# Attention and two expert layers on one core: a scheduler is told that three weight loads land later

## The chip, the core and the metric

The kernel runs on one core of a Trainium2 chip. The metric is the time of one execution on the device in microseconds, as the median of several runs. Engines are named as the profile names them: PE is TensorE (matmuls), PEld its weight loads, DVE VectorE, ACT ScalarE, POOL GpSimd and SP SyncE, whose queue issues the transfers (DMA). Each engine takes its instructions in the order in which the program emits them.

## What is computed

Three layers, one behind the other, in float32:

```python
for t in range(S):                       # attention: B=2, H=8, S=768, D=40
    C = f_stab * C + i_stab * outer(v[t], k[t]);  n = f_stab * n + i_stab * k[t]
    y[t] = sigmoid(o_gate[t]) * (C @ q[t]) / max(|n . q[t]|, 1)
x = y as 1536 tokens x 320
x = sum over 4 experts of p[:, e] * (relu(x @ w1[e]) @ w2[e])      # w1 320x1024, w2 1024x320
e = argmax(x @ w_gate), gate = softmax there                       # 8 experts, at most 384 tokens each
out[i] = gate[i] * (relu(x[i] @ w1[e]) @ w2[e])  for tokens that found a place, else 0
```

The first expert layer is called moe (experts k = 0 to 3), the second moe2 (k = 4 to 11, so k = 8 is moe2's expert 4).

## The kernel before

**Staging.** The attention is done in 12 units of 128 tokens, on PE up to about 200 us. Each unit leaves a token tile in xT. moe begins while the attention runs, an expert's tile at a time: layer 1 (L1, 128 matmuls of 128 columns in four quads at L652, or groups of four tiles in matmuls of 512 columns, also L652, with a closing half at L661), then layer 2 (L2, L674). Between them a bank is emptied twice: ACT takes the relu (L681), DVE the part that 16 bits have cut off (L683). DVE adds an expert's result to the accumulator (L715).

**Weights.** An expert's weights come from DRAM as float32 by `w_load`, w1 in three parts of 512 KB and w2 in two halves of 640 KB, into one buffer for each (`raw`). ACT passes over each piece for its largest value (L529), POOL reduces over the partitions, DVE spreads the result (L563) and makes a scale from it (L444 to L456). Then ACT (L597) and DVE (L602) split the weights into two 16-bit halves. Experts k = 8 to 11 come first in the order, and their halves are stored in DRAM and fetched again later (L506).

**Routing.** When a tile has its last moe expert, it is scaled and split (L633), transposed (by a transfer on SP, L640, or for the last three tiles by PE, L1432), and multiplied with the gate (L1441). PE counts how many tokens precede each one in its expert (L1467, L1468), and POOL scatters the rows into `disp` in DRAM. From there SP reads them back transposed (L1561 for three early expert tiles, L1768 for the window, which is the bulk of moe2). The results go out by indirect stores from POOL.

**What sets the order.** The kernel doesn't emit as it goes. Every operation is recorded by `Sched.add` with an engine, a cost in us and its dependencies. `Sched.starts` plays the program through with these costs and gives each operation a planned start; `run` emits the operations in order of planned start. A planned time isn't a measured one. It decides only what stands ahead of what in an engine's queue. Planned transfers of 1.44 to 1.9 us (the weight loads, 1.46 and 1.82) that end behind 165 us are taken to land `LOADS[0]` = 1.0 us later than the plain sum. Semaphores are derived from the dependencies, so that any order is right.

Of the kernel before, what the change touches and what calls it, by code (L numbers as in the profile page):

```python
# [67 lines left out]
LOADS = (1.0, 165.0)  # L68


class Sched:
# [86 lines left out]
    def starts(self, lst):  # L158
# [13 lines left out]
        while count < n:  # L172
            t, e = min((max(free[e], min(est[i] for i in c)), e) for e, c in ready.items() if c)
            i = min((i for i in ready[e] if est[i] <= t + self.HOLD[e]), key=lambda i: (i not in self.now, lst[i], i))
            ready[e].remove(i)
            if e == "DMA" and len(lanes) >= 8 and t < lanes[-8]:
                free[e] = lanes[-8]
                ready[e].append(i)
                continue
            start[i] = max(t, est[i])  # L180
            us = ops[i][1]
            count += 1
            free[e] = end = start[i] + us
            if e == "DMA":
                if ops[i][0] == "DMA":
                    free[e] = start[i] + 0.43
                    end = pipe = max(pipe, free[e]) + (us if us >= 0.8 else 0.15)
                else:
                    end = pipe = max(pipe, end)
                lanes.append(end + 1.7)  # L190
            if e == "DMA" and 1.44 < ops[i][1] < 1.9 and end > LOADS[1]:
                end += LOADS[0]
            for q in users[i]:
                est[q] = max(est[q], end + self.lag(ops[i][0], ops[q][0]) + self.care(ops[i][0], ops[q][0], end) + (SLACK if q in self.late else 0.0))
                left[q] -= 1
                if not left[q]:
                    ready.setdefault(unit[q], []).append(q)
# [1865 lines left out]
```

## Time and profile before

| | |
|---|---|
| median of 3 runs | 491.23 us (490.77 to 492.03) |
| profiled execution | 491.25 us, of which span 489.5 us |
| granted TensorE clock | 1.0 of full speed |
| PE busy | 473.4 us (97% of the span) |
| DVE, ACT, POOL busy | 342.4, 311.8, 144.5 us |
| moved by DMA | 89.10 MB |

The span is the time from the first to the last instruction of the profiled execution; the 1.75 us beside it are start and end. Busy is the time in which an engine had an instruction at work. Matmuls are pipelined and their ends are modelled. In timelines and waits, "a <-ACT b" is idle time that the named instruction ended.

### The profile page before, as it was taken

How to read it: one execution, taken by the hardware profiler on the slowest of the kernel's cores; microseconds unless marked ns; L12 is line 12 of the kernel's file. 1: busy time of each engine (PE TensorE's matmuls, PEld its weight loads, DVE VectorE, ACT ScalarE, POOL GpSimd, SP SyncE). 2: the span in 40 equal slices, each digit the busy share in tenths (PEclk: the TensorE clock that was granted, in tenths of full speed). 3: DMA queues.
4: the chain of work that ended last, by engine and by line, in shares of the span. 5: the costliest groups of instructions: out<-in, count | busy, mean ns of one | idle time of the engine just before them, and what ended most of it. 6: DMA issues, size and time to landing. Idle time of an engine off the chain costs nothing.

```text
span 489.5 us, 13777 instructions
## 1 busy us (share of the span) xinstructions
PE 473.4 (97%) x5469; PEld 363.0 (74%) x5469; DVE 342.4 (70%) x1008; ACT 311.8 (64%) x666; POOL 144.5 (30%) x297
## 2 busy tenths in 40 slices
PE   8999999999989899999999999999999999999995
PEld 6998978868878798887464646565564798978884
DVE  5898998799999934764978795679989882222110
ACT  1997979577687854866665678788978451312221
POOL 4742152664875420301102101010514121311111
PEclk9999999999999999999999999999999999999999
DMA  7996783354543796928887776627393464989301
GB/s 225 318 240 200 161 288 77 72 131 103 105 61 67 213 338 210 191 78 298 300 265 274 268 253 264 192 73 207 112 221 56 91 260 76 301 194 311 137 16 35
DMA packets 71588, 89.10 MB, mean 182 GB/s; under 512 B 49457, under 2 KB 57123, under 8 KB 71518
## 3 DMA queue, kind: packets, MB, share of 16 engines
q1 hardware_dynamic: 70318, 84.43, 60.6%
q0 software_dynamic: 1200, 3.73, 2.3%
q8 instruction: 45, 0.74, 0.6%
q14 instruction: 25, 0.20, 0.1%
HBM read 55.89 MB, written 21.70 MB: 159 GB/s over the span
## 4 chain that ended last, share of the span: by engine, by line
PE 51%; DVE 23%; DMA 17%; issue 6%; ACT 3%; POOL 0%; POOLq 0%; ACTq 0%; DVEq 0%; SPq 0%
PE po L674 20%; PE ph L652 14%; DMA out_dram<-acc,usm 9%; PE x L652 9%; DMA arena<-arena 3%; DVE arena L683 3%; DVE w L602 3%; DMA raw<-in_moe_w_dram 3%; DVE arena L1196 2%; DMA arena<-in_att_dram 2%; DVE arena L1066 2%; PE x L674 1%; PE ph L420 1%; ACT junk L529 1%; DVE usm L1005 1%
## 5 line engine op out<-in xcount | busy, mean ns | idle before, releaser
L674 PEld LDWEIGHTS <-arena 128*128 128x128 f16 (+1 forms) x1416 | 136.8, 98 | 53.9 <-issue 2.0
L652 PEld LDWEIGHTS <-w 128*128 128x128 f16 x1792 | 97.1, 98 | 5.0 <-issue 3.9
L652 PE MATMUL ph<-xT,w 128*128 128x128 f16 (+3 forms) x1664 | 96.2, 217 | 2.1 <-DVE arena L683 1.1
L652 PEld LDWEIGHTS <-arena 128*128 128x128 f16 x936 | 62.1, 98 | 39.6 <-issue 1.5
L674 PE MATMUL po<-arena 128*128 128x320 f16 x648 | 90.3, 299 | 0.0
L674 PE MATMUL po<-w,arena 128*128 128x320 f16 (+1 forms) x600 | 86.3, 299 | 1.4 <-DVE acc L715 1.3
L529 ACT ACTIVATE junk<-raw 128x512 bf16<-128x512 f32 (+1 forms) x105 | 69.7, 664 | 8.3 <-DMA raw<-in_moe_w_dram 6.6
L683 DVE SCALAR_TENSOR_TENSOR arena<-ph,arena 128x512 f16<-128x512 f32 x76 | 51.5, 682 | 15.0 <-ACT arena L681 14.9
L597 ACT ACTIVATE w<-raw,wsm 128x640 f16<-128x640 f32 (+1 forms) x56 | 50.4, 960 | 15.5 <-DVE wsm L451 15.5
L602 DVE SCALAR_TENSOR_TENSOR w<-raw,wsm,w 128x640 f16<-128x640 f32 (+1 forms) x56 | 57.1, 1049 | 4.3 <-ACT w L597 4.2
L681 ACT ACTIVATE arena<-ph 128x512 f16<-128x512 f32 x76 | 44.5, 588 | 20.4 <-PE ph L652 12.8
L652 PE MATMUL ph<-xT,arena 128*128 128x128 f16 (+4 forms) x472 | 57.5, 275 | 0.0
L652 PE MATMUL x<-xT,arena 128*128 128x128 f16 (+4 forms) x464 | 56.0, 274 | 0.0
L548 POOL CROSS_LANE_REDUCE wsm<-wsm 128x1 f32<-128x6 f32 (+1 forms) x24 | 9.7, 402 | 101.2 <-ACT junk L529 82.5
L602 DVE SCALAR_TENSOR_TENSOR arena<-raw,wsm,arena 128x640 f16<-128x640 f32 (+1 forms) x28 | 30.5, 1101 | 1.9 <-ACT arena L597 1.8
L715 DVE SCALAR_TENSOR_TENSOR acc<-po,cfs,acc 128x320 f32<-128x320 f32 x36 | 19.6, 545 | 14.8 <-PE po L674 13.5
L703 POOL TENSOR_TENSOR cfs<-pw,invx 128x1 f32<-128x1 f32 x48 | 17.8, 402 | 35.5 <-DVE invx L456 30.9
L597 ACT ACTIVATE arena<-raw,wsm 128x640 f16<-128x640 f32 (+1 forms) x28 | 25.7, 955 | 2.9 <-DVE wsm L451 2.9
L1806 POOL DMA_INDIRECT out_dram<-acc,usm x13 | 12.7, 974 | 48.4 <-ACT acc L1803 46.5
L681 ACT ACTIVATE arena<-x 128x512 f16<-128x512 f32 x26 | 14.5, 593 | 15.5 <-PE x L652 8.5
L1213 POOL TENSOR_TENSOR arena<-arena 128x512 f16<-128x512 f32 x16 | 20.6, 1304 | 12.1 <-ACT arena L1209 12.1
L1800 DVE SCALAR_TENSOR_TENSOR arena<-x,arena 128x512 f16<-128x512 f32 (+1 forms) x10 | 6.5, 652 | 25.2 <-ACT arena L1795 25.2
(245 smaller groups left out, 676.7 us busy)
## 6 DMA issues: line engine op xcount, KB each, us to landing
raw<-in_moe_w_dram SPq DMA_DIRECT2D x36, 512.0 KB
raw<-in_moe_w_dram SPq DMA_DIRECT2D x24, 640.0 KB
ws<-w SPq DMA_DIRECT2D x8, 768.0 KB
ws<-w SPq DMA_DIRECT2D x8, 640.0 KB
arena<-in_att_dram SPq DMA_DIRECT2D x8, 492.0 KB
disp<-zero SPq DMA_DIRECT2D x1, 3936.0 KB
arena<-ws SPq DMA_DIRECT2D x4, 768.0 KB
arena<-ws SPq DMA_DIRECT2D x4, 640.0 KB
```

The source lines that it names most:

```text
L529: nc.scalar.activation(out=junk[:, 0:w], in_=raw[:, i * w:(i + 1) * w], func=AF.Abs, accum_out=am[:, i:i + 1])
L597: lambda sl=sl: nc.scalar.activation(out=wh[:, sl], in_=raw[:, sl], func=AF.Copy, scale=sc),
L602: lambda sl=sl: nc.vector.scalar_tensor_tensor(wl[:, sl], raw[:, sl], sc, wh[:, sl], ALU.mult, ALU.subtract),
L652: nc.tensor.matmul(out=out, lhsT=wb[wi][:, c, f * 128:(f + 1) * 128], rhs=rhs(xc), start=(i == 0), stop=(i == LAST))
L674: nc.tensor.matmul(out=po[0:n, 0:DM], lhsT=hs[:, f, sl], rhs=ws[:, f, :], start=(f == 0 and i == 0), stop=(f == NF - 1 and i == 2),)
L681: act(0.52, lambda: nc.scalar.activation(out=hh, in_=ph, func=AF.Relu), [kp] + ex, [kh])
L683: 0.6, lambda: nc.vector.scalar_tensor_tensor(hl, ph, 0.0, hh, ALU.max, ALU.subtract),
L703: 0.26, lambda: nc.gpsimd.tensor_tensor(cf, pw[:, t, k:k + 1], invx[:, t:t + 1], ALU.mult),
L715: lambda: nc.vector.scalar_tensor_tensor(acc[:, t], po[:, 0:DM], cf, acc[:, t], ALU.mult, ALU.add),
L1066: lambda x=x, hi=hi, lo=lo, src=src: nc.vector.scalar_tensor_tensor(lo, src, sc[:, x:x + 1], hi, ALU.mult, ALU.subtract), [kr2, ks, key("h ...
L1213: 1.3, lambda j=j: nc.gpsimd.tensor_tensor(Wl[:, j::2], pb[:, j::2], Wh[:, j::2], ALU.subtract),
L1806: nc.gpsimd.indirect_dma_start(out=view_of(), out_offset=bass.IndirectOffsetOnAxis(ap=ix[0:n], axis=0), in_=acc[0:n, y], in_offset=None, b ...
```

## The change

One number in the scheduler's model: weight loads whose planned end lies between 191 and 205 us are taken to land 3.0 instead of 1.0 us behind the plain sum.

```diff
             if e == "DMA" and 1.44 < ops[i][1] < 1.9 and end > LOADS[1]:
-                end += LOADS[0]
+                end += LOADS[0] + (2.0 if 191.0 < end < 205.0 else 0.0)
             for q in users[i]:
```

Three loads fall in these bounds: the third part of w1 and both halves of w2 of expert k = 8. No instruction is added and none is left out, and no queue gets another kind of work. What moves is the order, from 205 to about 405 us behind the start.

On ACT, where expert k = 8's weights arrive (raw_87 is the buffer of w2, raw_86 that of w1, ph_97 and ph_98 are banks of layer 1); - is before, + is the change:

```order
 L681 ACTIVATE arena<-ph_97 128x512
 L529 ACTIVATE junk,wsm<-raw_86 128x512 x5
+L529 ACTIVATE junk,wsm<-raw_87 128x640
+L681 ACTIVATE arena<-ph_98 128x512
+L529 ACTIVATE junk,wsm<-raw_87 128x640
+L681 ACTIVATE arena<-ph_97 128x512
 L529 ACTIVATE junk,wsm<-raw_87 128x640 x2
-L681 ACTIVATE arena<-ph_98 128x512
-L529 ACTIVATE junk,wsm<-raw_87 128x640
-L681 ACTIVATE arena<-ph_97 128x512
-L529 ACTIVATE junk,wsm<-raw_87 128x640
 L681 ACTIVATE arena<-ph_98 128x512
```

The relu of bank ph_98 stood behind two passes over w2 and stands behind one; that of ph_97 stood behind three and stands behind two.

On PE, at the same place (x_102 is a bank that a group of four tiles of expert k = 2 uses, w_89 holds 16-bit weights of w1, po_100 a bank of layer 2):

```order
 L674 LDWEIGHTS arena
 L674 MATMUL po_100<-w_91,arena 128x320
+L652 LDWEIGHTS arena
+L652 MATMUL x_102<-xT,arena 128x512
...
 L652 LDWEIGHTS w_89
 L652 MATMUL ph_98<-xT,w_89 128x128
```

Seven such pairs, one block of layer 1, stand now ahead of the run of 128 matmuls on ph_98 and ph_97. Before, they stood behind that run and the 96 matmuls of layer 2 that follow it.

On DVE, behind the loads' arrival, the order of a bank's second emptying and of the scale of w2:

```order
 L715 SCALAR_TENSOR_TENSOR acc<-po_100,cfs,acc 128x320
 L683 SCALAR_TENSOR_TENSOR arena<-ph_97,arena 128x512
-L683 SCALAR_TENSOR_TENSOR arena<-ph_98,arena 128x512
-L563 STREAM_SHUFFLE wsm<-wsm 128x1
-L444 TENSOR_SCALAR wsm<-wsm 128x1
+L563 STREAM_SHUFFLE wsm<-wsm 128x1
+L444 TENSOR_SCALAR wsm<-wsm 128x1
+L683 SCALAR_TENSOR_TENSOR arena<-ph_98,arena 128x512
 L446 TENSOR_SCALAR wsm<-wsm 128x1
```

The emptying of ph_98 stands now behind two instructions of the scale.

Behind that the orders agree again up to the routing, from about 325 us on. There most engines' queues differ: sums and emptyings come ahead of weight splits of k = 5 to 7. On SP, the end of that stage (raw_87 and raw_86 loads of k = 6 and 7, L640 the transposes of token tiles):

```order
+L426 DMA raw_86<-in_moe_w_dram 128x1024 x3
+L640 DMA_TRANSPOSE arena<-arena 128x5x128
+L426 DMA raw_87<-in_moe_w_dram 128x1280
+L640 DMA_TRANSPOSE arena<-arena 128x5x128
 L426 DMA raw_87<-in_moe_w_dram 128x1280
 L640 DMA_TRANSPOSE arena<-arena 128x5x128 x2
-L426 DMA raw_87<-in_moe_w_dram 128x1280
-L640 DMA_TRANSPOSE arena<-arena 128x5x128 x2
-L426 DMA raw_86<-in_moe_w_dram 128x1024 x3
-L426 DMA raw_87<-in_moe_w_dram 128x1280 x2
-L640 DMA_TRANSPOSE arena<-arena 128x5x128 x4
```

Before, all five loads of k = 7 stood ahead of the last four transposes. In the change the first of these transposes stands behind the three loads of w1 and ahead of both of w2.

On PE, near the end of the routing (L1520 and L1467 count tokens, po_100 is a half of layer 2 of the first early tile, which runs under a branch, L1591):

```order
 L1520 LDWEIGHTS call
 L1520 MATMUL x_102<-run,call 128x8
-L1591 COMPARE_AND_BRANCH
-L674 LDWEIGHTS arena
-L674 MATMUL po_100<-arena 128x320
...
-L1591 UNCONDITIONAL_BRANCH x2
-L1467 LDWEIGHTS call
```

In the change these 12 matmuls stand one quad of layer 1 earlier, ahead of the count of token tile 9. The counts of tiles 10 and 11 have also one more block ahead of them, a quad of layer 1 or a half of layer 2 of the next early tiles.

## Rows read from the trace of the kernel before

**Rows 1.** The page: busy us (share of the span) and instructions of an engine.

```profile
PE 473.4 (97%) x5469; PEld 363.0 (74%) x5469; DVE 342.4 (70%) x1008; ACT 311.8 (64%) x666; POOL 144.5 (30%) x297
```

**Rows 2.** Waits of PE, 200 to 480 us: us in total, times, longest.

```profile
PE po L1840 <- issue: 1.2, 1, 1.2
PE ph L652 <- DVE arena L683: 0.9, 1, 0.9
PE x L652 <- issue: 0.5, 1, 0.5
PE x L1441 <- DMA arena<-arena: 0.4, 1, 0.4
```

**Rows 3.** The chain of waits, 198 to 236 us: start, us, what.

```profile
201.15 7.28 DMA raw<-in_moe_w_dram
...
208.52 0.84 ACT junk L529 x2
...
209.38 0.83 ACT junk L529 x2
210.21 0.49 ACT arena L681
...
210.72 0.70 DVE arena L683
...
231.81 1.51 PE ph L652 x7
```

**Rows 4.** Timeline of PE, 203 to 240 us: start, us, instruction.

```profile
207.19 3.42 PE L674 MATMUL po<-w,arena 128*128 128x320 f16 x24
211.47 7.31 PE L652 MATMUL ph<-xT,w 128*128 128x128 f16 x128 [0.86 <-DVE arena L683]
...
236.28 0.39 PE L661 MATMUL ph<-xT,arena 64*128 64x512 f16 x1
```

**Rows 5.** Timeline of DVE, 186 to 220 us.

```profile
202.25 0.88 DVE L602 SCALAR_TENSOR_TENSOR arena<-raw,wsm,arena 128x640 f16<-128x640 f32 x1
...
214.70 0.15 DVE L563 STREAM_SHUFFLE wsm<-wsm 128x1 f32<-128x1 f32 x1
214.89 0.15 DVE L444 TENSOR_SCALAR wsm<-wsm 128x1 f32<-128x1 f32 x1
```

**Rows 6.** Timeline of PE, 360 to 416 us.

```profile
366.23 0.28 PE L1441 MATMUL x<-wg,arena 128*128 128x16 f16 x5 [0.41 <-DMA arena<-arena]
...
392.38 0.27 PE L1441 MATMUL x<-wg,arena 128*128 128x16 f16 x5
...
398.81 1.79 PE L674 MATMUL po<-arena 128*128 128x320 f16 x12
400.43 0.17 PE L1467 MATMUL x<-run,call 128*128 128x8 bf16 x1
...
407.36 1.95 PE L652 MATMUL x<-xT,arena 128*128 128x128 f16 x32
...
414.20 1.31 PE L652 MATMUL x<-xT,arena 128*128 128x80 f16 x32
```

**Rows 7.** Timeline of SP, 345 to 416 us: the issue of transfers.

```profile
351.40 8.53 SPq L426 DMA_DIRECT2D raw<-in_moe_w_dram  x5
360.97 8.68 SPq L640 DMA_TRANSPOSE arena<-arena  x4
...
387.63 1.57 SPq L640 DMA_TRANSPOSE arena<-arena  x1
...
401.53 1.23 SPq L1561 DMA_TRANSPOSE xT<-disp  x1
407.56 3.84 SPq L1768 DMA_TRANSPOSE xT<-disp  x3
```

**Rows 8.** Slices of 0.5 us: busy by engine, clock, DMA share, GB/s.

```profile
403.50:404.00 0.50, 0.50 (x6) 0.35 (x4) 0.42 (x1) 0.00 (x0) 0.00 (x0) 1.00 1.22 306
404.00:404.50 0.50, 0.50 (x6) 0.36 (x5) 0.19 (x2) 0.00 (x0) 0.43 (x1) 1.00 0.13 40
```

## The prediction

> **What bounds the kernel now.** I read the busy times first. TensorE (PE) is busy for 473.4 of 489.5 us [rows 1], so before any reason to the contrary a microsecond that PE waits is a microsecond of the kernel, and anything that happens on another engine counts only when PE comes to wait for it. The second view is therefore the list of what PE waits for, from 200 us on, where the change acts [rows 2]. The reader is to see how short it is: 1.2 and 0.5 us with no releaser, 0.9 us for DVE's L683 and 0.4 us for a transfer of routed rows, L1441. The third view is the chain of waits around the 0.9 [rows 3], the fourth PE's timeline there [rows 4].
>
> They read so. The first half of moe2 expert 4's w2 lands at about 208.5. ACT then makes two passes over it for the maximum of its weights (0.84 and 0.83), the relu of a bank only after them (210.21), DVE the low half of the same bank (210.72, 0.70) [rows 3]. PE has ended its 24 matmuls at 207.19 + 3.42 = 210.61 and begins the next run at 211.47 [rows 4]. The wait of 0.86 is one pass of ACT in the wrong place of an in-order queue, not a lack of ACT.
>
> **The change, part by part.** No transfer is added, removed or made slower by the number itself: it only tells the scheduler that three loads land 2 us later, and the emitted order follows. So the cost is the cost of the order, in four parts.
>
> *ACT at 208.5.* One pass of L529 now stands ahead of the relu instead of two. The relu comes 0.83 earlier, at about 209.4, DVE's half at 209.9, and the bank is free at about 210.64 instead of 211.47 [rows 3]. The load itself is not touched: it was waited for with nothing ahead of it.
>
> *PE at 210.6.* The first block of seven matmuls on bank x_102 goes in front of the run of 128. Such a block is 1.51 us [rows 3]; its weights are those of expert 2, whose last split on DVE starts at 202.25 and lasts 0.88 [rows 5], so it can start at 210.61. The run of 128 is then wanted at 210.61 + 1.51 = 212.12, with its bank free 1.5 us before. The wait of 0.86 is gone by either of the two moves alone. From 212.12 to the old place of the block PE runs 0.65 us later than before, and behind it 0.86 earlier. **Term: -0.86.**
>
> *DVE behind it.* The low half of the next bank now stands behind the shuffle and L444 of the weights' scale. These start at 214.70 and 214.89 and last 0.15 [rows 5], so the half ends near 215.04 + 0.69 = 215.73, and PE wants its bank again two quads into its run. A run of 128 matmuls, four quads, is 7.31 us [rows 4], so that is at 212.12 + 3.66 = 215.78. It just fits. Bounds: nothing, and one half of 0.69 that would have to be waited for whole.
>
> *The routing stage, 325 to 405 us.* PE waits 0.41 at 366.23 for the rows of token tile 4 [rows 6]. SP issued that transpose at 360.97, behind five weight loads that it started at 351.40 [rows 7]. In the new order it stands ahead of the last two of these loads. **Term: -0.41**, if the transpose lands in its usual time. That time is bounded by two rows. The one at 401.53 has its data moved by about 404.1, 2.6 us after issue, where the share of the DMA engines falls from 1.22 to 0.13 [rows 7, 8]. The one at 387.63 was used without a wait at 392.38, so it takes at most 4.75 [rows 6, 7]; at 366.23 it took 5.26, with the loads in the same engines.
>
> In exchange, the first L2 half of the first early tile (12 matmuls at 398.81 [rows 6]) now runs before the count of tile 9 and so directly behind its own L1. It needs ACT's relu and DVE's low half of a bank of which PE ends just one L1 half (some 1.8 us) earlier. Relu and half together are 0.5 + 0.7 [rows 3], which fits, but DVE has the small operations of the routing in the same queue. Bounds: 0, and 0.69, one more half ahead. I take 0.2, nearer to nothing, as DVE's operations in that queue are short ones. **Term: +0.2**, which stands for the near miss at 215.7 too.
>
> The same exchange puts the 1.62 us of such a half (398.81 to the start of what followed it, 400.43 [rows 6]) ahead of the counts of tiles 9 and 11. Net of the gain of 1.07 that is left they come 0.55 later, and with them two groups of transposes that read the scattered rows. The third early tile's, issued at 401.53, goes to 402.08 and lands at 404.7 by the lower bound and 406.8 by the upper; PE wants it at 407.36 - 1.07 = 406.29 [rows 6, 7]. The window's, issued at 407.56, go to 408.11 and land at 410.7 to 412.9; PE wants them at 414.20 - 1.07 = 413.13 [rows 6, 7]. So the one costs 0 to 0.5 and the other nothing. I take nothing for both: for these same small transposes the row with the data's end is the nearer one.
>
> Weight splits of k = 5 to 7 move back on DVE behind the routing; that is what makes room for it, and their readers are in the window, behind 414. The last of them also frees the buffers into which the first window expert's stored halves are fetched; on SP that fetch stands behind the transpose of 387.63 [rows 7], so the split has to be later than this before it costs anything.
>
> Sum, against the profiled run's own 491.25 us (span 489.5 and 1.75 around it; the median of the runs is 491.23): 491.25 - 0.86 - 0.41 + 0.2 = **490.2 us**, 0.2% less. A measurement of this kernel can tell about 0.3%, 1.5 us, from no change, so this counts as no difference.
>
> **The rivals.**
> *The waits only move (chance 0.2).* PE is busy by a modelled end of pipelined matmuls, and it may be paced by its operands, so that a block begun 0.86 us earlier ends when it did. Then the time stays at 491.25. For it: weight loads are busy for only 363.0 us [rows 1], and 0.65 us of the first gain is paid in advance as lateness from 212 to 234. Against it: the chain of waits runs through PE alone behind 211.47, and a block of seven stands there at 1.51 [rows 3] without waiting for an operand.
> The Trainium skill, in "Perfetto Trace Analysis", section "Identifying the Most-Contended Engine", speaks for this rival: it says that matmul occupancy is no good measure of how near TensorE is to its limit, and that weight-load occupancy is to be read. By that, 74% and not 97% is the load of the engine [rows 1], and the sum would be this rival's 491.25. In this trace the listed waits of PE are 1.2 + 0.9 + 0.5 + 0.4 = 3.0 us in 280 [rows 2], which is no sign of a quarter to spare.
>
> *The window's rows come late (0.17), the other sign.* Place: the window's transposes on SP at 407.56, behind the last tile's count and scatter. It decides from 413.13 - 408.11 - 4.75 = 0.27 us of further lateness on; beyond that every microsecond costs one, and the kernel is slower than before from 0.27 + 1.07 = 1.34. For it: DVE is filled with routing, and the counts now stand behind one more block. If another L2 half (1.62) and another low half (0.69) stand ahead of that count in fact, the transposes land at 408.11 + 2.31 + 4.75 = 415.17, PE waits 2.04, and the time is **492.2**. Against it: if a transpose takes 2.6 us, more than 2 us are to spare.
>
> *More goes than I count (0.13).* The two stalls without a releaser, 0.5 and 1.2 [rows 2], stand behind conditional blocks whose order changes a little upstream. If both vanish the time is 490.2 - 1.7 = **488.5**. For it: nothing waits on data there. Against it: the instructions around them stay in the same order.
>
> **How the numbers follow.** The forecast has chance 0.5, with a range of its own of 489.3 (no loss, and 0.7 of the two stalls without a releaser gone) to 491.0 (0.5 at the third early tile, and 0.3 of the second gain not there). The range over all cases goes from 488.8 to 492.5, which cuts half of the fast rival and the far tail of the slow one. Faster by over 0.3% means below 489.76: most of the third rival and the lower part of the forecast's, 0.26. Slower by over 0.3% means above 492.70: the slow rival where it reaches further, 0.14. The rest, 0.60, is the same.
>
> **What would show it.** In the new profile ACT should have one L529 between 208.5 and the relu; PE should begin seven L652 matmuls into an x bank at about 210.6 with no wait, and the run of 128 at about 212.1. At 234 to 236 the same instruction (the first halves L661) should start about 0.86 earlier than 236.28 [rows 4]. The list of PE's waits should have lost L683's 0.9 and L1441's 0.4. A wait of PE on L683 near 215.8 or before an L2 block near 395 measures my 0.2. The prediction is wrong if a wait on transposed rows shows between 390 and 414, or if PE's stretch from 234 to 325, where PE's order is the same, takes a different time.

## The result and the profile after

| | before | after |
|---|---|---|
| median, 16 runs each beside each other | 490.9 us (488.7 to 492.8) | 493.19 us (491.8 to 498.0) |
| profiled execution | 491.25 us, span 489.5 | 492.03 us, span 490.2 |

The ratio is 1.0056 (95%: 1.0034 to 1.0078), so on this chip the change makes the kernel slower, by more than the 0.3% that can be told from no change. On four other chips, in the experiments, the same two kernels gave 1.0027 (0.9998 to 1.0057), 0.996 (0.9927 to 0.9992), 0.9959 (0.9935 to 0.9982) and 0.9969 (0.994 to 0.9998).

The work is the same. The page, busy us by engine:

```profile
PE 473.1 (96%) x5469; PEld 362.8 (74%) x5469; DVE 341.2 (70%) x1008; ACT 311.3 (64%) x666; POOL 142.7 (29%) x297
```

PE is as busy as before [rows 1], and its list of waits from 200 us on (total, times, longest) has other entries than that of [rows 2]:

```profile
PE po L1840 <- issue: 1.4, 1, 1.4
PE ph L652 <- DMA xT<-disp: 0.7, 1, 0.7
PE x L1441 <- DMA arena<-arena: 0.3, 1, 0.3
```

L683's 0.9 is gone, L1441's 0.4 has become 0.3, and a wait for transposed rows of 0.7 is new. First the place that the change is about, PE's timeline (start, us, instruction, and the idle time before it with what ended it) for [rows 3, 4], and ACT's under it:

```profile
206.59 3.42 PE L674 MATMUL po<-w,arena 128*128 128x320 f16 x24
209.85 1.67 PE L652 MATMUL x<-xT,arena 128*128 128x512 f16 x7
211.36 7.31 PE L652 MATMUL ph<-xT,w 128*128 128x128 f16 x128
...
234.66 0.39 PE L661 MATMUL ph<-xT,arena 64*128 64x512 f16 x1
```

```profile
206.18 0.74 ACT L529 ACTIVATE junk<-raw 128x640 bf16<-128x640 f32 x1 [0.36 <-DMA raw<-in_moe_w_dram]
...
208.28 0.60 ACT L681 ACTIVATE arena<-ph 128x512 f16<-128x512 f32 x1 [1.27 <-PE po L674]
208.77 0.73 ACT L529 ACTIVATE junk<-raw 128x640 bf16<-128x640 f32 x1
```

PE takes the block of seven at 209.85 and the run of 128 at 211.36, both without a wait, and the same instruction as in [rows 4] starts at 234.66 instead of 236.28: 1.62 us earlier. Of these, 0.60 were there before the place was reached (206.59 for 207.19), so the place gave 1.02. But look at ACT: w2 landed at 206.18 and held ACT up for only 0.36. The relu at 208.28 waited for PE, not for a pass of L529.

Now the routing and the window, PE and then SP, for [rows 6, 7]:

```profile
363.90 0.27 PE L1441 MATMUL x<-wg,arena 128*128 128x16 f16 x5
...
371.78 0.28 PE L1441 MATMUL x<-wg,arena 128*128 128x16 f16 x5 [0.30 <-DMA arena<-arena]
...
412.92 1.31 PE L652 MATMUL x<-xT,arena 128*128 128x80 f16 x32
...
415.21 1.89 PE L652 MATMUL ph<-xT,w 128*128 128x64 f16 x64
417.80 0.95 PE L652 MATMUL ph<-xT,arena 128*128 128x32 f16 x32 [0.70 <-DMA xT<-disp]
418.80 3.71 PE L674 MATMUL x<-arena 128*80 128x320 f16 x24
...
432.70 0.32 PE L1840 MATMUL po<-w,arena 128*32 128x320 f16 x3 [1.39 <-issue]
```

```profile
408.01 3.84 SPq L1768 DMA_TRANSPOSE xT<-disp  x3
...
412.52 4.39 SPq L1768 DMA_TRANSPOSE xT<-disp  x2
```

Tile 4's rows are there without a wait (363.90), and a transpose of a later tile is waited for instead, 0.30 at 371.78. At 412.92 the window begins 1.28 ahead of the old 414.20. At 417.80 PE waits 0.70 for the rows of a later transpose, and at 432.70 it stands 1.39 with no releaser (1.2 before [rows 2]). PE's last block begins at 480.44 for 480.97, still 0.53 ahead. The span is 0.7 longer nevertheless, for it ends 5.5 us behind the issue of the last transfer, an indirect store of POOL (484.70 to 490.2), and in before 4.3 behind it (485.23 to 489.5); in the experiments short and long ends stand under either order. So the longer span of this one execution isn't the change's work; what the change does is read from stretches of it.

### The profile page after: what moved, and what is told of

Read it like the earlier page. It is cut to its first block, busy times and chain, and to the rows that moved or that the text cites. A ratio compares the mean times of both kernels' runs of the same rounds, so it can differ in the third digit from the quotient of the medians.

```text
span 490.2 us, 13778 instructions
## 1 busy us (share of the span) xinstructions
PE 473.1 (96%) x5469; PEld 362.8 (74%) x5469; DVE 341.2 (70%) x1008; ACT 311.3 (64%) x666; POOL 142.7 (29%) x297
## 5 line engine op out<-in xcount | busy, mean ns | idle before, releaser
L652 PEld LDWEIGHTS <-w 128*128 128x128 f16 x1792 | 97.1, 98 | 4.1 <-issue 2.8
L652 PE MATMUL ph<-xT,w 128*128 128x128 f16 (+3 forms) x1664 | 96.2, 217 | 1.2 <-DVE usm L446 0.9
L652 PEld LDWEIGHTS <-arena 128*128 128x128 f16 x936 | 62.2, 98 | 40.5 <-issue 2.3
L529 ACT ACTIVATE junk<-raw 128x512 bf16<-128x512 f32 (+1 forms) x105 | 69.7, 664 | 6.6 <-DMA raw<-in_moe_w_dram 5.1
L683 DVE SCALAR_TENSOR_TENSOR arena<-ph,arena 128x512 f16<-128x512 f32 x76 | 51.5, 681 | 13.3 <-ACT arena L681 13.2
L652 PE MATMUL ph<-xT,arena 128*128 128x128 f16 (+4 forms) x472 | 57.6, 276 | 0.7 <-DMA xT<-disp 0.7
L652 PE MATMUL x<-xT,arena 128*128 128x128 f16 (+4 forms) x464 | 56.2, 274 | 0.0
L715 DVE SCALAR_TENSOR_TENSOR acc<-po,cfs,acc 128x320 f32<-128x320 f32 x36 | 19.6, 545 | 10.1 <-PE po L674 9.9
```

Source lines behind the costliest of these rows:

```text
L529: nc.scalar.activation(out=junk[:, 0:w], in_=raw[:, i * w:(i + 1) * w], func=AF.Abs, accum_out=am[:, i:i + 1])
L652: nc.tensor.matmul(out=out, lhsT=wb[wi][:, c, f * 128:(f + 1) * 128], rhs=rhs(xc), start=(i == 0), stop=(i == LAST))
L683: 0.6, lambda: nc.vector.scalar_tensor_tensor(hl, ph, 0.0, hh, ALU.max, ALU.subtract),
L715: lambda: nc.vector.scalar_tensor_tensor(acc[:, t], po[:, 0:DM], cf, acc[:, t], ALU.mult, ALU.add),
```

## The experiments

I matched the matmuls of all profiles by their number in PE's order and measured three stretches. In the table, **place** runs from matmul 2600 to 3600 (the first place and the rest of moe), **routing** from 3600 to 4340, **window** from 4340 to 4720 (about 416 to 436 us), and the next three columns are what the list of PE's waits has from 405 us to the end: waits with no releaser on L652 and on L1840, waits for the transposed rows xT, and waits for ACT's L1795. **Clock** is the lowest granted clock in a slice of 5 us between 405 and 445. Each chip was used for one set of runs, so that a chip can't be told from its set.

```
chip     run               order           place   routing window | L652 L1840  xT  L1795 | clock
(first)  before            old             140.21   75.52  18.39  |  0.5   1.2   -    -   | 1.00
(first)  after             new             139.21   75.86  19.13  |   -    1.4  0.7   -   | 1.00
13       before2           old             139.79   76.14  19.27  |  2.0    -    -    -   | 1.00
13       again             new             139.20   75.76  19.93  |  0.2    -   0.5  0.6  | 0.68
13       first             new, then old   139.20   76.06  20.20  |  2.0    -    -    -   | 0.80
13       last              old, then new   139.27   76.03  18.85  |   -    0.6  0.9  0.2  | 1.00
7        third             new             139.54   76.02  19.42  |  0.4   0.8  0.9  0.2  | 1.00
7        bpad              old, start cut  139.62   76.34  21.57  |  3.5    -    -    -   | 0.66
7        apad              new, start cut  139.20   75.31  16.97  |   -     -    -    -   | 1.00
7        counts            new, counts old 139.88   78.16  18.40  |   -    0.5  0.4  0.3  | 1.00
5        before4           old             140.36   75.16  16.74  |   -     -    -    -   | 1.00
5        after4            new             139.20   76.42  19.75  |   -     -   0.7  0.6  | 0.75
5        apad2             new, start cut  139.20   75.72  16.41  |   -     -   0.3   -   | 1.00
5        delay2            old, PE later     -      75.34  16.75  |   -    0.2   -    -   | 1.00
9        before5           old             140.31   75.82  20.44  |  2.4    -    -    -   | 0.66
9        after5            new             139.20   76.00  19.69  |  0.2   1.6  0.5  0.2  | 1.00
9        first2            new, then old   139.53   76.37  19.46  |  2.1    -    -    -   | 1.00
9        last2             old, then new   140.59   76.42  19.41  |  0.4   1.0  0.8  0.2  | 1.00
2        fetch_late        old, SP changed 139.20   76.27  20.47  |  2.2    -    -    -   | 0.76
2        first_fetch_late  as first, too   139.32   76.34  21.19  |  2.9    -    -    -   | 0.82
```

Read the window's column with the ones behind it. Without its listed waits the window is 16.1 to 17.4 us wherever the clock stayed at 1.00, and 18.0 to 18.9 where it fell (of bpad's 3.5, 0.8 lies behind the window). So the window's time is a floor that is much the same under either order, plus waits, plus some 1.4 us where the clock falls, the difference of the two means (17.0 and 18.4).

What the table leaves out spreads by more than the change moves. Matmul 2600, ahead of which the orders are the same but for the padding, is reached at 199.5 to 205.3 us, and from the end of the last matmul to the end of the span it is 5.1 to 5.2 us in ten profiles and 6.1 to 7.1 in the other ten, under either order. The whole time of a single profile therefore says little, and the stretches are compared.

The times, this kernel's median against the median of before on the same chip:

| run | chip | this | before | ratio (95%) |
|---|---|---|---|---|
| again (after) | 13 | 492.59 | 494.77 | 0.996 (0.9927 to 0.9992) |
| before2 (before) | 13 | 494.83 | 494.77 | 0.9996 (0.9973 to 1.0019) |
| first | 13 | 494.25 | 494.77 | 0.9987 (0.996 to 1.0014) |
| last | 13 | 494.56 | 494.77 | 1.0011 (0.9989 to 1.0034) |
| third (after) | 7 | 493.25 | 495.55 | 0.9959 (0.9935 to 0.9982) |
| bpad | 7 | 496.35 | 495.55 | 1.0019 (0.9986 to 1.0053) |
| apad | 7 | 491.09 | 495.55 | 0.9902 (0.9863 to 0.9941) |
| counts | 7 | 494.63 | 495.55 | 0.9983 (0.9956 to 1.0011) |
| after4 (after) | 5 | 491.76 | 490.61 | 1.0027 (0.9998 to 1.0057) |
| before4 (before) | 5 | 490.14 | 490.61 | 1.0006 (0.9977 to 1.0035) |
| apad2 | 5 | 490.86 | 490.61 | 1.001 (0.9981 to 1.0039) |
| delay2 | 5 | 489.38 | 490.61 | 1.0006 (0.9977 to 1.0035) |
| after5 (after) | 9 | 494.21 | 494.98 | 0.9969 (0.994 to 0.9998) |
| before5 (before) | 9 | 493.77 | 494.98 | 0.997 (0.9941 to 1.0) |
| first2 | 9 | 494.99 | 494.98 | 0.9985 (0.9957 to 1.0014) |
| last2 | 9 | 493.66 | 494.98 | 0.996 (0.9925 to 0.9994) |
| fetch_late | 2 | 495.18 | 494.46 | 1.0006 (0.9972 to 1.0041) |
| first_fetch_late | 2 | 494.1 | 494.46 | 0.9997 (0.9967 to 1.0026) |

A ratio here compares runs in equal conditions and isn't always the quotient of the medians beside it. One execution of first took 1714.62 us and is left out. Apad's median is of 6 executions, the others' of 12.

**Which half of the change does it: again, before2, first, last.** The new order was cut in two at 300 us of planned time. The program is played through with both numbers, and each operation takes its place from one of them:

```diff
-        start = self.starts(self.urgency())
+        s0, s1 = self.starts(lst, 0.0), self.starts(lst, 2.0)          # lst = self.urgency()
+        start = [y if x < 300.0 else 1000.0 + x for x, y in zip(s0, s1)]   # first
+        start = [x if x < 300.0 else 1000.0 + y for x, y in zip(s0, s1)]   # last
```

Again and before2 are the two kernels unchanged, for a profile of each on this chip.

> The changed kernel once more, unaltered, for a second profile and the spans of more executions. Theory W (the window's rows come late): PE waits for transposed rows (xT from disp) behind 412 us by 0.7 us or more, the median is 1.5 to 3 us above the kernel before, and the share of it lies between 405 and 425 us of the profile. Theory E (the end): PE ends its last matmul near 484 us as before, and the surplus lies behind it, in the last stores and the closing of the program, with longer spans going with a lower mean clock. Theory N (noise of the one profile): no difference beyond 0.5 us.

> The kernel before, unaltered, as a control and for a second profile. All theories: ratio 1.000 within 0.002. Theory E expects its span and clock to scatter less than those of the changed kernel; theory W expects no wait for transposed rows behind 400 us of more than 0.3 us.

> The new order for all operations that the scheduler plans ahead of 300 us, the old order behind: the weights' arrival near 210 us alone, with nothing changed in the routing. Prediction's own term: 0.86 us faster than before, ratio 0.998. Theory W: the same, 0.998, or a little of it lost at the window, 1.000. Theory E: undecided, between 0.998 and 1.005. If the first place is the cause of the loss: 1.005.

> The old order for all operations planned ahead of 300 us, the new one behind: the routing stage alone. Theory W: slower than before by 2 to 3 us, ratio 1.004 to 1.006, with the wait for transposed rows behind 405 us. Prediction's own terms: 0.2 us faster, 0.9995. If the first place is the cause of the loss: 1.000.

On this chip after is the faster one, and not for the reason in the prediction. None of the three theories forecast that: theory W has its wait in again (0.5, less than its 0.7) and in last (0.9), but not its time; theory E's late end comes under either order; theory N's half a microsecond is passed. The kernel before is at 494.8 here and at 490.9 on the first chip, after at 492.6 and 493.2. PE's timeline of before2 shows what had come in:

```profile
417.47 1.73 PE L652 MATMUL ph<-xT,w 128*128 128x64 f16 x48
419.68 0.28 PE L652 MATMUL ph<-xT,w 128*128 128x32 f16 x5 [0.48 <-issue]
420.41 0.28 PE L652 MATMUL ph<-xT,w 128*128 128x32 f16 x5 [0.45 <-issue]
421.15 0.30 PE L652 MATMUL ph<-xT,w 128*128 128x32 f16 x6 [0.46 <-issue]
421.88 0.96 PE L652 MATMUL ph<-xT,arena 128*128 128x32 f16 x32 [0.43 <-issue]
```

Four stalls of 0.43 to 0.48 with no releaser, 1.8 in all, between groups of five or six small matmuls. First has them too, last and again don't. They come with the old order of the window, and the first chip's profile of before doesn't show them. (The halves' times alone don't say which half did it: 0.9987 and 1.0011 for first and last, where the whole change is at 0.996.) Conversely last shows what the new order does in the window (PE's waits, 405 to 480 us):

```profile
PE ph L652 <- DMA xT<-disp: 0.9, 1, 0.9
PE po L1840 <- issue: 0.6, 1, 0.6
PE x L674 <- ACT arena L1795: 0.2, 1, 0.2
```

The first place is also seen without the change. With the old order there, ACT waited for w2 2.11 us in before, 1.68 in before2 and 0.55 in last; PE's wait for L683 was 0.86 [rows 4], 0.4 and none (ACT in before, ACT and PE in before2):

```profile
208.52 0.74 ACT L529 ACTIVATE junk<-raw 128x640 bf16<-128x640 f32 x1 [2.11 <-DMA raw<-in_moe_w_dram]
```

```profile
208.87 0.74 ACT L529 ACTIVATE junk<-raw 128x640 bf16<-128x640 f32 x1 [1.68 <-DMA raw<-in_moe_w_dram]
```

```profile
PE ph L652 <- DVE arena L683: 0.4, 1, 0.4
```

**Is it the place of the counts, or of the code: third, bpad, apad, counts.** Third is after once more. Bpad and apad are before and after with 64 of the start's filler matmuls of 256 columns cut into two of 128, so that all that follows on PE stands 128 instructions (64 matmuls and their weight loads) further back in its program. Counts is after with PE's counts of tiles 9 to 11 put back ahead of the early tiles' blocks:

```diff
-            nc.tensor.matmul(out=bank[name][:, 0:256], lhsT=zero16[:, 0:128], rhs=zero16[:, 0:256], ...)
+            # bpad, apad: for the first 64, two of these with 128 columns
+        start[2114] = s1[2039] + 0.001                        # counts: recorded operations 2114, 2090,
+        start[2090], start[2119] = s1[2066] + 0.001, s1[2066] + 0.002   # 2119, 2115 and 2122 placed
+        start[2115] = s1[2099] + 0.001; start[2122] = s1[2133] + 0.001  # behind the named ones
```

> The changed kernel, unaltered, in another session. The comparison so far was 1.0056 in one session and 0.996 in the next, the kernel before being the one that moved (490.9 and 494.8 us). Theory I (PE's supply of instructions in the window stage decides, and how it falls differs by session): a ratio anywhere from 0.995 to 1.006, the changed kernel itself again at 492 to 494 us. Theory W (the window's rows are late in the changed order, always): ratio 1.003 or more here, and the last session is an exception.

> The kernel before with 64 of PE's first filler matmuls (256 columns) each cut into two of 128: no work more, 128 PE instructions more ahead of everything else. PE fetches its instructions 256 at a time. Theory I: the stalls without a releaser in the window stage, which stood at matmuls 4546 and 4674 of the program (128 matmuls with their weight loads apart, 256 instructions), move by 64 matmuls in the program, to about 4482 and 4610, and the time changes by up to 2 us either way. Theory W: they stay with their instructions, time within 0.5 us of the kernel before.

> The changed kernel with the same 128 additional PE instructions at the start. Theory I: its stalls behind 415 us stand at other matmuls than in the changed kernel, time 490 to 495 us. Theory W: the wait of 0.7 us for the transposed rows at about 417 us stays at its matmul, and the time is that of the changed kernel within 0.5 us.

> The changed kernel with one part of its order put back: the counts of tiles 9 to 11 stand again ahead of the early tiles' blocks that had come in front of them on PE, as in the kernel before. Theory W: the window's transposes are issued some 1.6 us earlier relative to PE, the wait for xT from disp behind 415 us (0.5 to 0.9 us in the profiles so far) is gone, and the kernel is 0.5 to 1 us faster than the changed one. Theory I: the wait is gone, but stalls without a releaser stand in its place and the time is within 0.5 us of the changed kernel.

Third's 0.9959 is against theory W, which wanted 1.003 or more. Both theories expected counts to lose the wait for rows, and it didn't. Counts shows the price of the other side. Its wait for rows falls to 0.4, and PE waits for the counts themselves (waits, 390 to 425 us):

```profile
PE x L1467 <- DVE cnei L1531: 0.7, 1, 0.7
PE x L1467 <- DVE arena L1454: 0.6, 1, 0.6
PE ph L652 <- DMA xT<-disp: 0.4, 1, 0.4
PE x L1467 <- DVE run L1471: 0.4, 1, 0.4
```

2.1 us are lost in the routing (78.16 for third's 76.02) for half a microsecond of this wait (0.9 in third). PE comes to the counts before DVE has what they count, so their place isn't the loss by itself.

Bpad, whose profiled execution is its longest (499.67 us), keeps the old order's stalls in the same run of matmuls (4370 to 4388, numbered as in before, where before2 has 4365 to 4381), though all of them stand 64 matmuls later in the program, so these aren't tied to a position in PE's program. Another one did move, though not to 4610, the place that "Theory I" gave it:

```profile
443.42 1.23 PE L652 MATMUL x<-xT,arena 128*128 128x128 f16 x19 [0.77 <-issue]
```

In the eight unpadded profiles that have the gap of L1840 it stands at matmul 4674 (to within one). This one, counted from bpad's own start with its 64 matmuls more, is at 4802, just 128 matmuls or 256 instructions further. The traces say what goes with it. They list a DMA queue of instructions (queue 8) with 45 packets of 16 KB, which at 256 instructions each fit PE's 10938 matmuls and weight loads. In the eight profiles matmul 4674 starts 1.5 to 1.8 us behind the end of the last such packet, in bpad the one at 4802 1.4 behind it. In the nine unpadded profiles without the gap it starts 2.5 to 4.2 us behind that end, but for before4 (1.8, with 0.08 of idle time). That fits a PE that stands until its next instructions are there; it wasn't tried by itself.

Apad has neither wait nor stall in the window, and is the fastest kernel of this study on this chip. Its windows against those of again, both with the new order (us, busy by engine, granted clock, DMA share, GB/s):

```profile
410.00:420.00 10.00, 8.89 (x188) 7.53 (x186) 2.25 (x7) 2.62 (x7) 1.91 (x4) 0.99 0.80 114
420.00:430.00 10.00, 9.77 (x171) 8.63 (x170) 1.42 (x3) 1.72 (x3) 2.38 (x3) 0.84 1.09 344
```

```profile
410.00:420.00 10.00, 10.00 (x215) 9.09 (x213) 1.68 (x5) 2.41 (x5) 0.45 (x3) 1.00 0.69 87
420.00:430.00 10.00, 9.80 (x196) 8.78 (x193) 2.77 (x5) 3.11 (x7) 3.83 (x4) 1.00 0.98 344
```

PE of apad is busy 19.80 of 20 us. In again it lost 1.1 us in the first slice, and the granted clock of the second is 0.84. PE's timeline of again shows the order of events:

```profile
417.26 0.95 PE L652 MATMUL ph<-xT,arena 128*128 128x32 f16 x32 [0.50 <-DMA xT<-disp]
418.76 5.38 PE L674 MATMUL x<-arena 128*80 128x320 f16 x24 [0.55 <-ACT arena L1795]
```

Two stalls in 1.5 us, then 24 matmuls of layer 2 in 5.38 us that take 3.71 in after at full clock. Stalls as long aren't always followed by a fall of the clock: before2 and first2, with four stalls each, keep 1.00.

**The chips on which before is quick: after4, before4, apad2, delay2.** Chip 5 is like the first one (before at 490.6). Delay2 is before with nine more matmuls of 512 columns, whose product is overwritten, at about 310 us, to bring PE later to the window; nine fillers are merged away at the start.

```diff
-        for i, (wi, c, xc) in enumerate(L1_PAIRS[:n]):
+        for j, (i, (wi, c, xc)) in enumerate([(0, L1_PAIRS[0])] * more + list(enumerate(L1_PAIRS[:n]))):   # more = 9, once
```

> The changed kernel, unaltered, on another chip. So far it was at 493.2, 492.6 and 493.3 us and the kernel before beside it at 490.9, 494.8 and 495.6. If the first comparison was the exception: ratio 0.994 to 0.998 again. If the sign is open from one set of runs to the next: anything from 0.994 to 1.006, mainly by where the kernel before stands.

> The kernel before as a control, for its third profile. Ratio 1.000 within 0.002. From the first matmul of the window's second group to PE's last window stage behind it (matmuls 4340 to 4720) it took 18.4 us in its first profile and 19.3 in the second; if it stands at 494 to 496 us here too, that stage should be near 19.3 or above, if at 491 near 18.4.

> The changed kernel with 128 additional PE instructions at the start, once more: it was at 491.1 us (ratio 0.990) with no wait of PE in the window stage. If the place of the instructions is what took the stalls away, it is below the changed kernel again by 1 to 2 us and the stage from matmul 4340 to 4720 takes 17 to 18 us. If that was chance, it stands within 0.5 us of the changed kernel.

> The kernel before with nine matmuls of 512 columns added to one block of layer 1 of expert k = 3 (1.95 us of PE at about 310 us, ahead of the routing), and nine filler matmuls at the start merged away, so that all later PE instructions keep their number; the added products are overwritten, the output is the same. The prediction's premise (PE's time ahead of the routing goes to the end one for one): 1.95 us slower, ratio 1.004. If the window stage takes up lead and lateness: 0 to 1 us slower, ratio 1.000 to 1.002.

Before4's window has no listed wait at all. After4 has the new order's waits and is the slower of the two, as on the first chip. Apad2 is level with before: its window (16.41) is as short as that of before4 (16.74), so what is gained over the unpadded after is the window's waits (its listed 0.3 is for the third early tile's rows, ahead of the window). It is 0.9 below after4, where 1 to 2 were expected. Before4's window is below the 18.4 expected of it, for it has no gap at L1840. Delay2's time, 1.0006 where the premise of the prediction gives 1.004, doesn't show its 1.95 us. In its profile routing and window (75.34 and 16.75) are those of before4 (75.16 and 16.74), so they don't take the lateness up; but matmul 2600 comes at 199.49 there, which is within the spread of that place, and whether the changed start did this isn't shown. It adds a third profile of the old order without the stalls.

**The sign once more, by halves: after5, before5, first2, last2.** Chip 9, the kernels of the first group.

> The changed kernel beside its two halves. Its stage from matmul 4340 to 4720 takes 18.9 to 19.9 us again, with a wait for xT from disp at matmul 4381. If the kernel before stands near 491 us here: ratio 1.002 to 1.006; if near 495: 0.995 to 0.998.

> The kernel before. If it stands near 491 us: the stage from matmul 4340 to 4720 takes 16.7 to 18.4 us and has no row of short stalls near matmul 4365; if near 495: 19 us and more, with four stalls of some 0.6 us from one matmul to the next between 4361 and 4388.

> New order ahead of 300 us (planned), old order behind, once more. If the loss is the routing's order: this kernel has the stage of the kernel before and is faster than it by 0 to 1 us (ratio 0.998 to 1.000), and faster than the changed kernel where the kernel before is. If the loss came from the first place: 1.003 and more where the changed kernel is slower.

> Old order ahead of 300 us, new order behind, once more. If the loss is the routing's order: the stage from matmul 4340 to 4720 as in the changed kernel, 18.9 us or more; where the kernel before stands near 491 us this one is slower by 1 to 2.5 us (1.002 to 1.005), where near 495 the same or faster. If the loss came from the first place: 1.000 in either case.

In the profiles it is the picture of chip 13 again, as the expectations had it: four stalls with the old order behind 300 us (before5, first2), the waits for rows with the new one (after5, last2). The times settle less here: before5, the same kernel as the one it is compared with, came out at 0.997 too, so that 0.9969 on this chip can't be told from no change.

The stalls are not all that the slow chips show. In all seven profiles there that have the old routing (before2, first, bpad, before5, first2, and the two of the next group) PE also waits 0.62 to 0.71 us for DVE's L1485 at matmul 4087, some 20 us ahead of the stalls, because DVE and ACT were released 1.3 to 1.7 us late, by what the trace calls remote and can't name. In the three with the old order on the quick chips (before, before4, delay2) there is neither. That stretch takes 0.8 us more, and the run of small matmuls with the stalls 2.7 to 3.0.

**Are the stalls the stored halves' fetch: fetch_late, first_fetch_late.** In the old order SP fetches the first stored halves from 416.7 us on (before2), and the stalls follow from 419.2 on. Here these four fetches stand behind the next window transpose, in before and in first:

```diff
+        start[2188], start[2189], start[2190], start[2191] = (start[2185] + 0.001 * j for j in range(1, 5))
```

> The kernel before with one change on SP: the four fetches of stored weights in the window stage stand behind the next window transpose instead of ahead of it, some 1.3 us later. If the fetches' traffic makes the short stalls: none near matmul 4365, the stage from matmul 4340 to 4720 takes 16.5 to 18.4 us, and where the kernel before stands near 495 us this one is 1 to 2.5 us faster (0.995 to 0.998), where near 491 the same. If the stalls have another cause: they stay where the kernel before has them, ratio 1.000.

> The same change on SP together with the new order ahead of 300 us and the old order behind. If the lead of 1 us from the first place can be kept once the window stage is free of the short stalls: 1 us faster than the other kernel here, ratio 0.993 to 0.998 to the kernel before. If the lead is lost in the stage anyway: the same as the other kernel.

SP and PE of fetch_late:

```profile
421.21 2.01 SPq L506 DMA_DIRECT2D arena<-ws  x4
```

```profile
422.22 0.25 PE L652 MATMUL ph<-xT,w 128*128 128x32 f16 x4 [0.50 <-issue]
422.93 0.21 PE L652 MATMUL ph<-xT,w 128*128 128x32 f16 x2 [0.46 <-issue]
423.68 0.23 PE L652 MATMUL ph<-xT,w 128*128 128x32 f16 x3 [0.53 <-issue]
424.40 0.47 PE L652 MATMUL ph<-xT,w 128*128 128x32 f16 x11 [0.49 <-issue]
```

The fetch starts 1.0 us ahead of the first stall instead of 2.9 (416.74 and 419.68 in before2), and the stalls stay in the same run of matmuls (4361 to 4370; 4364 to 4381 in first and before2), 0.46 to 0.53 each, and four. They don't follow the fetch, as one of the expectations has it. Its last packets are still under way beside them, so that it has no part in them at all isn't shown. First_fetch_late has four as well (0.23 to 1.39) and is at 0.9997, so its lead from the first place isn't seen in its time.

## Why the prediction was wrong

**The order moved as said; the sum didn't.** Each instruction stands and starts about where the steps put it: no wait at the first place, 1.62 us of lead at 234 to 236, tile 4 without its wait, the window's first transpose at 408.01 (forecast 408.11), PE ready for it at 412.92 (413.13). From 234 to 236 on PE's stretch to 325 takes the same time in both, so the rival "The waits only move" is out. The rule that I had put beside that rival, from the Trainium skill's "Perfetto Trace Analysis", section "Identifying the Most-Contended Engine" (matmul occupancy is no good measure of how near TensorE is to its limit), may hold elsewhere; here PE carried 1.62 us of lead through these 90 us whole, as an engine does that sets its own pace.

**The step that failed: the window's transposes at no cost.** I checked the first of them against the first block that reads it, and it did fit: it landed at 410.84 in after, 2.83 us behind its issue. But SP issues more, one behind the other, and PE stopped at the fourth: the matmul at 417.80 waits for the fourth's semaphore, and the trace has the fourth's last part landing at 417.76. The working that was missing uses two views that I had read only at their first rows, SP's and PE's timelines of before (the first line is the fourth and the fifth):

```profile
412.07 3.64 SPq L1768 DMA_TRANSPOSE xT<-disp  x2
```

```profile
416.49 1.89 PE L652 MATMUL ph<-xT,w 128*128 128x64 f16 x64
418.23 0.95 PE L652 MATMUL ph<-xT,arena 128*128 128x32 f16 x32
```

Before, the fourth was issued at 412.07 and landed at 415.94, 3.87 later and 2.29 ahead of PE's 418.23. In after it was issued at 412.52 and landed at 417.76, 5.24 later, which is more than the 4.75 that was my upper bound. PE begins that block 1.74 behind the run of 64 matmuls (418.23 - 416.49), so in after it would have begun it at 415.21 + 1.74 = 416.95 and lost 0.81, of which the list shows 0.70, for it counts from a modelled end. From 2.29 to spare to 0.81 lacking is 3.10: 1.28 of PE's lead, 0.45 for a later start on SP, and 1.37 for a transpose that took longer.

The traces also show what goes with the longer one. The first three transposes land 2.7 to 3.1 us behind their issue in all unpadded profiles. The fourth stands behind a load of many small pieces (usm, from 411.45 in before) and takes 3.7 to 3.95 in nine of the ten profiles with the old order and in both padded ones with the new, but 4.5 to 5.3 in the eight unpadded ones with the new order. In these eight a packet of PE's instructions (16 KB, queue 8) starts 1.5 to 2.6 us behind the fourth's issue (in after at 414.58). In the unpadded ones with the old order it starts 3.6 or more behind it (415.71 in before), when the fourth has all but landed, and the fifth is hit; only in first2 it comes at 3.45, and there the fourth takes 5.47, unnoticed behind the stalls. In a half microsecond while the packet is under way the DMA share, the time that the transfers took against that of 16 engines, is 3.0 and 3.2 at some 200 GB/s, in after and then in before:

```profile
415.30:415.80 0.50, 0.50 (x24) 0.50 (x21) 0.00 (x0) 0.00 (x0) 0.00 (x0) 1.00 3.02 199
```

```profile
416.00:416.50 0.50, 0.50 (x20) 0.50 (x17) 0.00 (x0) 0.50 (x3) 0.00 (x0) 1.00 3.19 211
```

The padding bears this out: with the code 128 instructions further back, the packet comes 2.8 to 2.9 us ahead of the fourth's issue in apad and apad2, the first three transposes are the slow ones (3.3 to 4.3), the fourth takes 3.8, and PE waits for none of them. So PE's lead did two things that the prediction had at nothing: it brought PE to the fourth transpose earlier, and, with the later start on SP, an instruction packet into that transpose.

So the rival "The window's rows come late" is what happened, in its queue but at a later transpose, and with 0.70 where I had given 2.04. A wait of 0.4 to 0.9 for these rows stands in all eight unpadded profiles with the new order in the window, each time ended 0.04 us behind the fourth's landing, and in none of the ten with the old one. Behind it come 0.2 to 0.6 for ACT's L1795 in seven of the eight.

**The later start.** Ahead of the window's transposes stand POOL's scatters of the rows. The last two in after:

```profile
403.70 0.97 POOL L1490 DMA_INDIRECT disp<-arena  x1 [4.16 <-DVE arena L1481]
404.97 0.98 POOL L1490 DMA_INDIRECT disp<-arena  x1 [0.31 <-issue]
```

The first of these two waited 4.16 us for DVE's L1481. In before the two begin at 402.12 and 404.07, so the last one is 0.90 later, and SP's first transpose 0.45. The rival spoke of DVE's queue here; that DVE's part behind a count is late because the counts stand one block later on PE fits this, and wasn't tried by itself.

**The term of -0.86 was one execution's.** The wait existed in the profile I had, since w2 landed 2.11 us late for ACT in it. In the nine profiles with the old order there, PE waits for L683 in two (0.86 and 0.4). The mean of the place is 139.92 us with the old order (8 profiles, without delay2) and 139.33 with the new one (11): the gain is 0.6. The larger part of it comes from elsewhere. In five of the nine PE waits 0.26 to 0.76 at 275 to 281 us for a sum of DVE (L715), in the eleven with the new order twice, 0.16 and 0.18. In before4, DVE and then PE:

```profile
278.71 1.55 DVE L534 TENSOR_REDUCE wsm<-raw 128x1 f32<-128x640 f32 x2 [2.90 <-DMA raw<-in_moe_w_dram]
```

```profile
280.77 3.42 PE L674 MATMUL po<-arena 128*128 128x320 f16 x24 [0.76 <-DVE acc L715]
```

The sum stands on DVE behind two passes for the largest weight (L534), and these wait 2.90 us for a load, in after4 0.40. It was said ahead of the prediction that the orders agree from the first place to about 325 us. PE's do, but ACT's and DVE's differ from 235 us on, in splits, passes and scales of weights, so the change acts here too; which of these moves brings the load earlier wasn't tried.

**The term of -0.41 was none.** A wait for one of L640's transposes only changed its tile: with the old order it stands at tile 4 in seven profiles of ten (0.19 to 0.42), with the new one at a later tile in seven of ten (0.30 to 0.56). The routing takes 75.2 to 76.4 under the old order and, without counts, 75.3 to 76.4 under the new one. **The +0.2 for near misses** was not needed: the list of after's waits has no L683.

**"More goes than I count"** didn't come: of the two stalls without a releaser the 0.5 went, and the 1.2 became 1.4. They don't belong to the order where I saw them: the one of L1840 goes with the instruction packets.

**The sign.** Routing and window together take 93.9, 91.9 and 92.1 us with the old order on the two chips where before runs in about 491 us, and 95.0 and 96.2 with the new one. That is 2.9 more, 2.1 of it in the window and 0.8 in the routing (means of three and of two profiles, which differ by 2.0 and 1.2 among themselves). 0.6 is gained at the first place, and 2.3 and 1.2 were measured (493.19 - 490.9, 491.76 - 490.61). On chips 13 and 9, where before runs in about 495, its stalls make the same stretch 95.4 to 96.3 (mean 95.9 of four), the new order takes 94.9 to 95.8 (mean 95.5 of four), and with the 0.6 of the first place that is 1.0 less; measured were 2.2 less (494.77 - 492.59) and 0.8 (494.98 - 494.21, which can't be told from nothing); on chip 7 it was 2.3 less (495.55 - 493.25), without a profile of the unpadded before. So the sign is accounted for on the slow chips by what the old order has there, the stalls and the wait at matmul 4087, the size only roughly. The kernel after is at 491.8 to 494.2 on all five chips, before at 490.6 to 495.6: it is mostly before that moves.

**What stays open.** What makes the stalls of the old order and the late release ahead of them, on four chips of six and on no other; the stalls follow neither the fetch nor a position in PE's program. Why an instruction packet slows the transposes beside it. And whether apad is better everywhere: it was 0.9902 (0.9863 to 0.9941) on chip 7, and 1.001 (0.9981 to 1.0039) on chip 5.

## What to carry to other kernels

A stall that one profile shows before the change is a sample; take a second profile before its whole length becomes a term, above all where a transfer's landing sets it. Where the waiting engine gets ahead, check each transfer of the queue that feeds it and not the first alone: here the first had time to spare and the fourth had none. An engine that gets ahead also has its instruction packets come earlier, and here one of them fell into a transfer that was waited for. Compare the orders of all engines, not that of the busiest alone. A difference of half a per cent can change its sign from chip to chip, so compare on several.

## What the runs showed of the hardware

- The same program differs between the six chips (one set of runs on each) by up to 1% (before: 490.6 to 495.6 us). What the profiles show of it, with the old order, is four or five stalls of PE of some 0.45 us (one of 1.4), without a releaser, in one run of small matmuls, and 20 us ahead of them a release of DVE and ACT that comes 1.3 to 1.7 us late.
- A gap of 0.2 to 1.6 us without a releaser stands at matmul 4674 in eight unpadded profiles, and one of 0.77 at 4802 where 64 matmuls more stood ahead. It ends 1.4 to 1.8 us behind the end of a 16 KB packet of the instruction queue, one for some 256 instructions, so a packet that comes late is the likely cause; it wasn't tried by itself.
- A small transpose from DRAM (the window's first three) landed 2.7 to 3.1 us behind its issue in the unpadded profiles, and up to 4.3 in the padded ones, where an instruction packet came among the three. The fourth, behind a load of small pieces, took 3.7 to 3.95 without such a packet in its first 3.5 us and 4.5 to 5.5 with one.
- After a group of stalls PE's granted clock fell to its lower level, 1.2 GHz (0.5 of full speed), in seven profiles (0.68 over 5 us in again), and windows in which it fell were some 1.4 us longer; in others with stalls of the same size it stayed at 2.4 GHz (before2, first2).
- The span ended 4.3 us behind the issue of the last indirect store in before and apad, 5.5 in after, 5.8 in bpad and 6.3 in again; the spread is as large as what the change moves.
